# A fused retention and feed-forward kernel: one batch's transposes go from TensorE to the DMA, and its rows are worked off one group later

## Chip, cores and metric

One core of one Trainium2 chip. The metric is the device time of one execution in microseconds (us). Every ratio is the mean time of one kernel's fast runs over the mean of the fast runs of the kernel before in the same rounds, with a 95% interval, so it is not quite the ratio of the medians that are quoted beside it. A run counts as slow when it is over 1.5% above the fastest of the same kernel. The granted clock is the share of TensorE's full clock that the profile shows as allowed.

## The reference, cut to what matters

Four batches, eight heads, 768 positions and a head dimension of 64 go through a decayed linear attention. Its result (3072 rows of 512) goes through an RMS normalisation and a gated feed-forward network (FFN) with an inner width of 1536.

```python
def _attn_ref(q, k, v):
    ...
    for t in range(S):
        state = gamma[None, :, None, None] * state + np.einsum('bhd,bhe->bhde', k[:, :, t], v[:, :, t])
        y[:, :, t] = scale * np.einsum('bhd,bhde->bhe', q[:, :, t], state)

def _moe_ref(x, w_gate, w_val, w_out, rms_g):
    xn = x / np.sqrt(np.mean(x * x, axis=-1, keepdims=True) + 1e-06) * rms_g
    g = xn @ w_gate
    return (g * (1.0 / (1.0 + np.exp(-g))) * (xn @ w_val)) @ w_out
```

## The kernel before: the parts that matter here

The 768 positions are cut into six chunks of 128. A chunk of one batch, say (1,3) for chunk 1 and batch 3, passes through small pieces: load q, k, v (`load`), transpose q and k (`piece_t`), scores (`piece_a`), output and state (`piece_y`), scale of the norm (`piece_rstd`), normalise (`piece_n`), transpose for the FFN (`piece_x`). Group c is the FFN of chunk c for all four batches, which is 512 columns: twelve rows of gate and value matmuls (`gv`), then the down projection (`down`). The pieces of chunk c+1 are slotted between the rows of group c. For chunks 0 and 1 the transposes are done on TensorE, from chunk 2 on by the DMA:

```python
def piece_t(c, b):
    d = cur[c, b]
    if c > 1:
        for n in "qk":
            t = work.tile([128, NHP, 128], BF16, name=n + "T", bufs=8)
            nc.sync.dma_start_transpose(out=t, in_=d[n + "b"])
            d[n + "T"] = t
        return
    # ... else: eight transposes on TensorE into qk_ps, one copy into qkT

def piece_rstd(c, b):        # on GpSimd (POOL), in the same queue as the loads
    ms = work.tile([128, 1], F32, name="ms")
    nc.gpsimd.tensor_scalar(out=ms, in0=cur[c, b]["ssq"], ...)
    rstd = work.tile([128, 1], F32, name="rstd")
    nc.gpsimd.tensor_tensor(out=rstd, in0=ms, in1=mhalf, op=ALU.pow)

def piece_n(c, b):
    ...
    if c > 1:
        nc.vector.scalar_tensor_tensor(out=xn, in0=x, scalar=d["rstd"], in1=g_bc,
                                       op0=ALU.mult, op1=ALU.mult)
        nc.sync.dma_start_transpose(out=cur[c, "xnT"][:, :, b * C:(b + 1) * C], in_=xn)
        return
    # ... else: xn = x * rstd; piece_x transposes it on TensorE and applies g_col

def second(n):               # the first two rows of group 1
    gv(n, t=slice(0, GT - C))            # three batches, 384 columns
    if n == 0:
        piece_x(1, B - 1)                # xn of (1,3), on TensorE
    else:
        gv(0, 2, slice(GT - C, GT))      # the fourth batch of both rows, packed

AHEAD0 = {1: ((L, 1, 1),), 5: ((W, 0, 0),), 6: ((L, 1, 2),), 8: ((W, 0, 1),), 9: ((L, 1, 3),),
          10: ((W, 0, 2), (L, 2, 0)), 12: ((L, 2, 1),), 13: ((T, 2, 0),), 14: ((L, 2, 2),), 15: ((T, 2, 1),),
          16: ((L, 2, 3, "qk"),), 17: ((L, 2, 3, "v"),), 23: ((T, 2, 2),)}
```

`AHEAD0` says what is issued ahead in each slot of group 0: L loads a chunk and batch, T transposes it, W loads a third of the output weights. Loads are issued by POOL, transposes and outputs by SyncE (SP).

## Time and profile before

| | before |
|---|---|
| median of the first six runs | 234.71 us |
| profiled span, granted clock | 232.5 us, 1.0 |
| first row of group 1 starts | 58.32 us |
| last load of chunk 2 (v_f of (2,3)) issued, landed | 55.13, 67.43 us |
| first row of group 2 starts | 93.70 us |
| its last xnT transpose landed | 93.34 us |

The prediction shows the lines that carry the argument. From 33 us on TensorE (PE) has no gap. The DMA is full up to about 70 us. The transposes for group 2 land only 0.36 us before PE wants them (93.70 - 93.34).

### The profile page before, as it was taken

The numbers are of one execution on the slowest core, as the hardware profiler recorded it, in microseconds if no ns is written. First come the engines' busy times: TensorE is split into PE (matmuls) and PEld (weight loads), VectorE is DVE, ScalarE is ACT, GpSimd is POOL, SyncE is SP. The second block draws the span as 40 slices with busy tenths as digits, with TensorE's granted clock in tenths as the row PEclk, the third lists the DMA queues.
The fourth block names the chain that finished last, engine by engine and source line by source line (L and its number), as shares of the span: only waits on it lengthen the run. The fifth ranks groups of instructions, "written<-read, shape, count | busy, mean of one in ns | idle before, by whom it ended". The sixth has DMA issues, their size and how long they took to land.

```text
span 232.5 us, 4395 instructions
## 1 busy us (share of the span) xinstructions
PE 223.4 (96%) x1662; PEld 121.1 (52%) x1687; DVE 130.5 (56%) x220; ACT 93.6 (40%) x185; POOL 120.2 (52%) x181
## 2 busy tenths in 40 slices
PE   6789999999999999999999999999999999999994
PEld 4567567565645554445554445554445554444443
DVE  6775454998548892249793239793238582243300
ACT  7444676646533332433432332433332432433221
POOL 8969978787537789374749374649200211000000
PEclk9999999999999999999999999999999999999999
DMA  8999999999999799899895599697400025100022
GB/s 138 178 198 205 203 193 204 211 198 161 157 233 187 83 137 240 210 120 173 119 157 137 159 114 149 104 124 190 140 3 0 0 48 162 64 0 1 3 90 90
DMA packets 89013, 30.70 MB, mean 132 GB/s; under 512 B 78560, under 2 KB 84448, under 8 KB 88992
## 3 DMA queue, kind: packets, MB, share of 16 engines
q0 software_dynamic: 55488, 16.78, 69.8%
q1 hardware_dynamic: 32832, 13.57, 29.0%
q8 instruction: 13, 0.21, 0.4%
q10 hardware_dynamic: 672, 0.07, 0.2%
q14 instruction: 8, 0.07, 0.1%
HBM read 28.58 MB, written 6.29 MB: 150 GB/s over the span
## 4 chain that ended last, share of the span: by engine, by line
PE 86%; DMA 6%; POOL 4%; issue 1%; ACT 1%; DVE 1%; POOLq 0%; ACTq 0%
PE o_ps L400 25%; PE v_ps L349 25%; PE g_ps L349 25%; DMA wv_b<-in_moe_w_val_dram 3%; PE a_ps L215 3%; PE y_ps L233 2%; DMA kb<-in_k_dram 2%; PE y_ps L238 2%; PE kv_ps L264 2%; PE o_ps L390 1%; POOL qb L75 1%; POOL kb L75 1%; POOL v_f L75 1%; PE qk_ps L204 1%; PE xt_ps L306 1%
## 5 line engine op out<-in xcount | busy, mean ns | idle before, releaser
L354 DVE TENSOR_TENSOR hT<-sg,v_ps 128x512 bf16<-128x512 bf16 (+2 forms) x76 | 50.0, 658 | 77.8 <-PE v_ps L349 64.1
L349 PE MATMUL v_ps<-xnT,wv_b 128*128 128x512 bf16 (+3 forms) x343 | 74.1, 342 | 0.6 <-DMA wv_b<-in_moe_w_val_dram 0.3
L349 PE MATMUL g_ps<-xnT,wg_b 128*128 128x512 bf16 (+3 forms) x338 | 73.8, 342 | 0.7
L353 ACT ACTIVATE sg<-g_ps 128x512 bf16<-128x512 f32 (+2 forms) x76 | 43.6, 573 | 64.9 <-PE g_ps L349 60.0
L400 PE MATMUL o_ps<-wo_b,hT 128*128 128x512 bf16 x266 | 62.0, 379 | 0.5
L349 PEld LDWEIGHTS <-wv_b 128*128 128x128 bf16 x348 | 31.6, 98 | 31.3 <-DMA wv_b<-in_moe_w_val_dram 0.7
L349 PEld LDWEIGHTS <-wg_b 128*128 128x128 bf16 x348 | 30.2, 98 | 27.4 <-DVE xnT L307 0.7
L400 PEld LDWEIGHTS <-hT 128*128 128x128 bf16 x276 | 26.2, 98 | 28.5 <-DVE hT L354 0.2
L278 POOL TENSOR_SCALAR ms<-ssq 128x1 f32<-128x1 f32 x24 | 5.8, 241 | 49.5 <-ACT xsq L248 49.3
L75 POOL DMA_DIRECT2D qb<-in_q_dram x23 | 21.4, 931 | 11.6 <-PE v_ps L349 7.2
L221 DVE TENSOR_TENSOR am<-a_ps,causal 128x512 bf16<-128x512 f32 x40 | 24.9, 680 | 0.2
L405 ACT COPY o_sb<-o_ps 128x512 f32<-128x512 f32 x23 | 13.2, 583 | 29.1 <-PE o_ps L400 23.0
L248 ACT ACTIVATE xsq<-x 128x512 f32<-128x512 f32 x20 | 12.6, 630 | 29.9 <-DVE x L244 28.0
L182 POOL TENSOR_TENSOR vp<-v_f,vdec 128x512 bf16<-128x512 f32 x18 | 18.5, 1052 | 6.5 <-DMA v_f<-in_v_dram 6.3
L75 POOL DMA_DIRECT2D v_f<-in_v_dram x23 | 21.1, 917 | 0.4 <-issue 0.3
L75 POOL DMA_DIRECT2D kb<-in_k_dram x23 | 20.5, 890 | 0.6 <-PE v_ps L349 0.4
L244 DVE TENSOR_TENSOR x<-y_ps,ydec 128x512 f32<-128x512 f32 x20 | 13.7, 685 | 2.3 <-PE y_ps L238 2.0
L289 DVE SCALAR_TENSOR_TENSOR xn<-x,rstd,g_bc 128x512 bf16<-128x512 f32 x16 | 12.6, 786 | 3.5 <-POOL rstd L281 3.5
L281 POOL TENSOR_TENSOR rstd<-ms,mhalf 128x1 f32<-128x1 f32 x24 | 13.4, 557 | 2.0
L233 PEld LDWEIGHTS <-am 128*128 128x128 bf16 x192 | 8.8, 98 | 4.5
L274 POOL CAST st_b<-st_f 64x256 bf16<-64x256 f32 x24 | 10.5, 438 | 0.7
L256 DVE TENSOR_TENSOR st_f<-st_f,kv_ps 128x512 f32<-128x512 f32 x16 | 10.8, 676 | 0.0
(72 smaller groups left out, 149.3 us busy)
## 6 DMA issues: line engine op xcount, KB each, us to landing
v_f<-in_v_dram POOLq DMA_DIRECT2D x23, 256.0 KB, 6.7
out_dram<-o_sb SPq DMA_DIRECT2D x23, 256.0 KB, 2.3
qb<-in_q_dram POOLq DMA_DIRECT2D x23, 128.0 KB, 6.5
kb<-in_k_dram POOLq DMA_DIRECT2D x23, 128.0 KB, 6.4
wg_b<-in_moe_w_gate_dram POOLq DMA_DIRECT2D x4, 384.0 KB, 7.8
wv_b<-in_moe_w_val_dram POOLq DMA_DIRECT2D x4, 384.0 KB, 9.3
wo_b<-in_moe_w_out_dram POOLq DMA_DIRECT2D x3, 512.0 KB, 10.0
q_f<-in_q_dram SPq DMA_DIRECT2D x1, 256.0 KB, 3.6
```

The lines of the kernel that those rows point to most:

```text
L75: i = nc.gpsimd.dma_start(out=x, in_=dict(q=q, k=k, v=v)[n][b].rearrange("h (c p) d -> c p h d", p=C)[c])
L182: (nc.vector if (c, b) in VECTOR_V else nc.gpsimd).tensor_tensor(out=d["vp"], in0=d["v_f"], in1=vdec[:, c, :, None].to_broadcast([128, H, ...
L221: nc.vector.tensor_tensor(out=am[:, i], in0=a_ps[i], in1=mask, op=ALU.mult)
L233: nc.tensor.matmul(y_ps[:, h, :], d["am"][:, i, hp, :], d["vp"][:, h, :], start=first, stop=last, skip_group_check=True)
L244: nc.vector.tensor_tensor(out=x, in0=y_ps, in1=ydec[:, c, :, None].to_broadcast([128, H, D]), op=ALU.mult)
L248: nc.scalar.activation(xsq, x.rearrange("p h d -> p (h d)"), AF.Square, accum_out=ssq)
L281: nc.gpsimd.tensor_tensor(out=rstd, in0=ms, in1=mhalf, op=ALU.pow)
L349: cur["mm"] = nc.tensor.matmul(ps[:, n - n0, :], w_b[:, s, n * 128:(n + 1) * 128], xnT[:, s, t], start=s == 0, stop=s == KS - 1)
L353: nc.scalar.activation(sg, g_ps, AF.Silu)
L354: nc.vector.tensor_tensor(out=hT[:, n0:n1, t], in0=sg, in1=v_ps, op=ALU.mult)
L400: nc.tensor.matmul(o_ps, hT[:, n, b * C:(b + 1) * C], wo_b[:, n, :], start=n == 0, stop=n == NFF - 1)
L405: nc.scalar.copy(o_sb, o_ps)
```

## The change

Its intent is to take twelve transposes of batch (1,3) off the engine that bounds the kernel. q, k and the normalised xn of that batch go through the DMA. Its scores and output move from the end of group 0 into group 1. To give them time, group 1 does eight rows for three batches only (384 columns) and packs the fourth batch's part of these rows (128 columns, 64 matmuls: "the packed fourth") in after them. The DMA-transposed xn needs the norm's gain in a row layout (`g_bc`), so that load moves from group 1 to the start. The diff, cut to its core:

```diff
+    LATE = (1, B - 1)
...
     def piece_t(c, b):
-        if c > 1:
+        if c > 1 or (c, b) == LATE:
...
     def piece_n(c, b):
-        if c > 1:
+        if c > 1 or (c, b) == LATE:
...
-        def second(n):
-            gv(n, t=slice(0, GT - C))
-            if n == 0:
-                piece_x(1, B - 1)
+        def second(i):
+            if i < 6:
+                for n in ((0,), (1,), (2,), (3, 4), (5,), (6, 7))[i]:
+                    gv(n, t=slice(0, GT - C))
+            elif i < 8:
+                gv(4 * (i - 6), 4 * (i - 5), slice(GT - C, GT))
             else:
-                gv(0, 2, slice(GT - C, GT))
+                gv(i)
+            for f in {0: (piece_a,), 2: (piece_y,), 3: (piece_n,)}.get(i, ()):
+                f(*LATE)
...
-     ... 13: ((T, 2, 0),), ...
+     ... 13: ((T, 1, 3), (T, 2, 0)), ...
-    AHEAD1 = {0: (...), 1: ((T, 1, 3),), 3: ((V, 1, 3),), 4: ((L, 2, 0),), ...
+    AHEAD1 = {0: (...), 4: ((T, 1, 3), (V, 1, 3)), 5: ((L, 2, 0),), ...
...
-            if c == 1 and i == 4:
+            if c == 0 and i == NFF:
                 nc.sync.dma_start(out=g_bc, in_=moe_rms_g.partition_broadcast(128))
```

More of the change, by code (lines that the diff above doesn't have):

```diff
@@ L316 @@
     PLAN = dict(a=(5, 5, 9, 9), y=(7, 8, 11, 12), n=(9, 10, 13, 13))
-    PLAN1 = dict(v=(9, 12, 14, 17), t=(9, 11, 13, 16), a=(10, 12, 15, 18), y=(11, 14, 17, 20),
-                 n=(13, 16, 19, 22), x=(15, 18, 21, None))
+    PLAN1 = dict(v=(9, 12, 14, 17), t=(9, 11, 13, None), a=(10, 12, 15, None), y=(11, 14, 17, None),
+                 n=(13, 16, 19, None), x=(15, 18, 21, None))
     def attention(c):
@@ L373, in first @@
                 f(*x)
-        def second(n):
-            gv(n, t=slice(0, GT - C))
-            if n == 0:
-                piece_x(1, B - 1)
-            else:
-                gv(0, 2, slice(GT - C, GT))
+        def second(i):
[4 more added lines that the diff above has]
+                gv(4 * (i - 6), 4 * (i - 5), slice(GT - C, GT))
+            else:
+                gv(i)
+            for f in {0: (piece_a,), 2: (piece_y,), 3: (piece_n,)}.get(i, ()):
+                f(*LATE)
+            if i == 3:
+                cur.pop(LATE)
         o_t = {}
@@ L408, in ffn @@
         for n in range(NFF):
-            slots.append(lambda n=n: first(n) if c == 0 else second(n) if c == 1 and n < 2 else gv(n))
+            slots.append(lambda n=n: first(n) if c == 0 else second(n) if c == 1 else gv(n))
         if c == 0:
@@ L445 @@
     AHEAD0 = {1: ((L, 1, 1),), 5: ((W, 0, 0),), 6: ((L, 1, 2),), 8: ((W, 0, 1),), 9: ((L, 1, 3),),
-              10: ((W, 0, 2), (L, 2, 0)), 12: ((L, 2, 1),), 13: ((T, 2, 0),), 14: ((L, 2, 2),), 15: ((T, 2, 1),),
+              10: ((W, 0, 2), (L, 2, 0)), 12: ((L, 2, 1),), 13: ((T, 1, 3), (T, 2, 0)), 14: ((L, 2, 2),), 15: ((T, 2, 1),),
               16: ((L, 2, 3, "qk"),), 17: ((L, 2, 3, "v"),), 23: ((T, 2, 2),)}
-    AHEAD1 = {0: ((V, 1, 0), (V, 1, 1), (V, 1, 2)), 1: ((T, 1, 3),), 3: ((V, 1, 3),),
-              4: ((L, 2, 0),), 6: ((L, 2, 1),), 8: ((L, 2, 2),), 9: ((L, 2, 3),), 10: ((T, 2, 0),),
+    AHEAD1 = {0: ((V, 1, 0), (V, 1, 1), (V, 1, 2)), 4: ((T, 1, 3), (V, 1, 3)),
+              5: ((L, 2, 0),), 6: ((L, 2, 1),), 8: ((L, 2, 2),), 9: ((L, 2, 3),), 10: ((T, 2, 0),),
               13: ((V, 2, 0),), 14: ((V, 2, 1), (T, 2, 1)), 15: ((V, 2, 2), (V, 2, 3), (T, 2, 2))}
```

## The prediction

> **What bounds the kernel now.** I read, in this order, the busy shares, the 40 slices, the chain of work that ended last, the groups by shape, then the timeline from 25 to 95 us.
>
> ```profile
> PE 223.4 (96%) x1662; PEld 121.1 (52%) x1687; DVE 130.5 (56%) x220; ACT 93.6 (40%) x185; POOL 120.2 (52%) x181
> PE   6789999999999999999999999999999999999994
> DMA  8999999999999799899895599697400025100022
> PE 86%; DMA 6%; POOL 4%; issue 1%; ACT 1%; DVE 1%; POOLq 0%; ACTq 0%
> ```
>
> TensorE (PE) is the bound: from the fourth slice it shows no idle tenth, and the chain is 86% PE. The rest of the chain, DMA and POOL, lies before 33 us. But the DMA row is also full for the first dozen slices (to about 70 us), exactly where the change works. So a PE instruction removed is worth its start-to-start time, and a PE wait added is lost in full.
>
> The timeline of PE at the start of group 1 (columns: start us, us, engine, line, operation, tile, count) gives the spacing:
>
> ```profile
> 58.32 0.81 PE L349 MATMUL g_ps<-xnT,wg_b 128*128 128x384 bf16 x4
> 58.97 0.81 PE L349 MATMUL v_ps<-xnT,wv_b 128*128 128x384 bf16 x4
> 59.62 0.39 PE L306 MATMUL xt_ps<-ident,xn 128*128 128x128 bf16 x4
> ...
> 61.14 0.61 PE L349 MATMUL g_ps<-xnT,wg_b 128*128 128x128 bf16 x8
> 61.59 0.61 PE L349 MATMUL v_ps<-xnT,wv_b 128*128 128x128 bf16 x8
> ...
> 62.90 1.03 PE L349 MATMUL v_ps<-xnT,wv_b 128*128 128x512 bf16 x4
> ```
>
> Read the differences of the starts, not the durations, which overlap. Four 384-column matmuls take 58.97 - 58.32 = 0.65 us, eight of 128 columns 61.59 - 61.14 = 0.45 us (56 ns each), and four of 512 columns 0.865 us (62.90 to 63.76, the next group's start). Four transposes of xn take 0.22 us (59.62 to 59.84). Nothing is idle between.
>
> **What the Trainium skill says.** "TensorE: Matmul & The Clock Gate", section "Wait — 56ns, not 53.3ns?", gives a warm start-to-start of N / 2.4 GHz plus about 2.5 ns. The trace agrees: 56 ns for 128 columns, 216 ns for 512. So cutting a row into 384 + 128 costs only the added fixed parts. "DMA: Bandwidth & Descriptors", section "Issuing engines are not separate DMA queues", says that DMAs from SP and GpSimd share the same 16 engines and interleave. The trace agrees: between 50 and 60 us transposes issued by SP took 8.0 to 10.9 us to land, while in the quiet stretch 158 to 162 us they took 2.5 us. The same page, section "Anatomy of one DMA — SWDGE (gpsimd) path", says that a semaphore wait is done by the issuing sequencer and that the DMA engines only drain their queues. So a transfer with no wait starts as soon as its instruction is reached, whatever its place in the program text. No run yet shows it for g_bc.
>
> **The change part by part.**
> Removed from PE: eight transposes of q and k of batch (1,3), 8 x 56 = 0.44 us, and four of its xn, 0.22 us. Together 0.67 us.
> Added to PE: eight rows are cut into 384 + 128 instead of two. A cut row costs 2 x 0.65 + 0.445 = 1.745 us against 2 x 0.865 = 1.73 us for a whole one, so 0.015 us more; six more rows cost 0.09 us. Net PE work: -0.57 us.
> Removed elsewhere: an ACT copy of 1.01 us, a DVE eviction of 0.68 us; the xn operation becomes 0.74 instead of 0.48 us. Neither engine binds, so 0.
> Moved: scores (about 0.43 us with its gap), y and kv (0.68 us) of batch (1,3) go from the end of group 0 to slots 0 and 2 of group 1. With the q,k transposes (0.44) the end of group 0 becomes 1.55 us shorter.
> Added to DMA: two transposes near 46 us and one near 67 us. The hardware queue used 29.0% of 232.5 us, 67 us, for 13.57 MB; by bytes a 0.13 MB transpose is an estimated 0.65 us of all 16 engines.
> Moved in DMA: g_bc (256 KB). In the built kernel it is the fourth instruction of SP with no wait, so I expect it near 3 us instead of 69.5, among the first loads.
>
> Three waits can be exposed.
>
> (a) xn of batch (1,2). Its scale comes from GpSimd (POOL), which issues five loads in a row before it:
>
> ```profile
> 49.14 0.56 POOL L281 TENSOR_TENSOR rstd<-ms,mhalf 128x1 f32<-128x1 f32 x1
> 49.66 0.95 POOL L75 DMA_DIRECT2D qb<-in_q_dram  x1
> 50.61 0.89 POOL L75 DMA_DIRECT2D kb<-in_k_dram  x1
> 51.47 0.92 POOL L75 DMA_DIRECT2D v_f<-in_v_dram  x1
> 52.35 0.91 POOL L75 DMA_DIRECT2D qb<-in_q_dram  x1
> 53.38 0.88 POOL L75 DMA_DIRECT2D kb<-in_k_dram  x1
> 54.34 0.19 POOL L278 TENSOR_SCALAR ms<-ssq 128x1 f32<-128x1 f32 x1
> 54.61 0.56 POOL L281 TENSOR_TENSOR rstd<-ms,mhalf 128x1 f32<-128x1 f32 x1
> ```
>
> ```profile
> 55.20 0.48 DVE L296 TENSOR_SCALAR xn<-x,rstd 128x512 bf16<-128x512 f32 x1 [0.35 <-POOL rstd L281]
> 56.37 0.39 PE L306 MATMUL xt_ps<-ident,xn 128*128 128x128 bf16 x4
> ```
>
> POOL is busy without a pause, so xn is ready at 55.68 whatever PE does. Now PE comes at 56.37, 0.69 us later. In the changed kernel the same five loads stand before the same ms, and PE has lost all of the 1.55 us before this point: it arrives at 54.82. It must wait until about 55.75: +0.93 us. This I trust most; it eats the whole gain (-0.57 + 0.93 = +0.36).
> The loads also wait for earlier loads. With two more transposes in a full DMA, v_f of (2,0), landing at about 52.9, may come up to a microsecond later and hold the kb load that was issued at 53.38: I put +0.3 us.
>
> (b) g_bc at the start. PE already waits there for a weight load:
>
> ```profile
> 27.27 0.82 PE L349 MATMUL v_ps<-xnT,wv_b 128*128 128x384 bf16 x4 [0.27 <-DMA wv_b<-in_moe_w_val_dram]
> ```
>
> 256 KB at the 200 GB/s of these slices is 1.3 us, at the near 370 GB/s of 65 to 68 us 0.7 us. If the backlog lasts to 27 us it comes out here in full; I put +0.4 us for what reaches PE.
>
> (c) xnT of the late batch. Counting from a group start at 57.70: row 0, scores, rows 1 and 2 to 62.1; y and kv to 62.8; x (0.68), square (0.82) and rstd (0.75) to about 65.3; DVE is then held by the product of row 4, so xn is done at about 66.9. The packed fourth is wanted after eight rows (10.4), 1.1 of batch (1,3) and about 0.8 for two score pieces of chunk 2: 57.70 + 12.3 = 70.0. That leaves 3.1 us. Later xnT pairs landed in 2.5 to 6.2 us. In front of it on SP is this:
>
> ```profile
> 61.42 4.65 SPq L190 DMA_TRANSPOSE kT<-kb  x1
> ...
> 69.53 0.57 SPq L471 DMA_DIRECT2D g_bc<-in_moe_rms_g_dram  x1
> ```
>
> That kT took 8.9 us to land, at 70.3. So the wait is between 0 and 2 us; I put +0.4, leaning on the author having chosen eight rows to give it time.
>
> Sum: -0.57 + 0.93 + 0.3 + 0.4 + 0.4 = +1.46 us, on 234.76: **236.2 us**.
>
> **The rivals.**
> R1, all waits stay hidden: only the 0.57 us shows, 234.2 us. For it: PE is gapless, and the eight rows look chosen for the purpose. Against it: the POOL chain of (a) does not shorten.
> R2, only (a) bites: 234.76 + 0.36 = 235.1 us. For it: that chain is there line by line, while the DMA terms are guesses.
> R3, DMA becomes the bound for a stretch: (a) grows to 2, (b) to 0.7, (c) to 2 us: -0.57 + 4.7, 238.9 us. For it: a full DMA row and landings of 9 to 12 us. Against it: transposes share one queue behind each other, so they cannot take much at a time.
>
> **Range and chances.** The low end, 234.4, is R1 with the spread of the runs (234.32 to 235.98). The high end, 238.2, lies short of R3. Two per cent is 4.7 us: faster needs a gain eight times the removed work, 0.01; slower needs more than R3, 0.03; within, 0.96.
>
> **What would show it.** PE matmul busy time down by some 0.5 us. The first idle mark of PE after 50 us on xt (line 309), from DVE xn, about 0.9 us or more, with POOL busy before it. g_bc issued by SP near 3 us. A wait on wv_b near 27 us above 0.27. A wait of the first 16-fold 128-column g_ps in group 1 on the xnT transpose, 0 to 2 us. Groups 2 to 5 unchanged. I am wrong if xt does not wait (then POOL ran earlier than I hold) and the time falls by half a microsecond; or if the scores of (1,3) wait for qT and kT, which I expect to land by 57 us, two before they are wanted.

## The result, and the profile after

| | before | after |
|---|---|---|
| median of six runs | 234.71 us | 248.51 us |
| lowest and highest | 234.32, 235.98 | 242.33, 250.91 |
| ratio of fast runs | | 1.0349 [1.0291, 1.0407] |
| fast runs, their clock | all six | 242.33 and 243.76, clock 1.0 |
| the other five runs of after (one beyond the six) | | 246.75 to 250.91, clock 0.993 to 0.977 |

The changed kernel is slower by 3.5% in its fast runs, about 8.2 us. These are only two of seven; its median is 5.9% above that of before. The profile of after fell on its slowest run (250.91 us, clock 0.977). So the page shows where the waits are, but their sizes are read, as far as possible, from the experiments. The profiles of e5 and e7 below are of slow runs too.

The page of after (busy time and recorded instructions, PE, granted clock and DMA by fortieths of the span, shares of the chain):

```profile
PE 229.5 (92%) x1723; PEld 125.7 (50%) x1723; DVE 129.2 (52%) x220; ACT 92.8 (37%) x185; POOL 120.1 (48%) x181
PE   7679999996982999969999999999999999999994
PEclk9999999999997799979999999999999999999999
DMA  7999999999999929978999799999720004400022
PE 71%; DMA 16%; POOL 5%; ACT 2%; issue 2%; DVE 1%; POOLq 0%; ACTq 0%; DVEq 0%
```

PE now has holes in slices 10, 12, 13 and 18, and the clock falls in three slices that lie in or just behind the last two holes. The chain's DMA share went from 6% to 16%. Busy time is no measure of work here: a matmul at half clock counts twice, and some matmul records are missing from the page of before.

PE's timeline of after at the four places where it waits (start, us, engine, line, operation, tile, count, idle before and releaser; lines of the changed file are three higher):

```profile
9.64 0.40 PE L201 MATMUL qb_ps<-ident,qb 128*128 128x128 bf16 x4 [1.52 <-DMA qb<-in_q_dram]
...
59.08 0.40 PE L309 MATMUL xt_ps<-ident,xn 128*128 128x128 bf16 x4 [2.27 <-DVE xn L299]
...
79.48 1.89 PE L352 MATMUL g_ps<-xnT,wg_b 128*128 128x128 bf16 x16 [5.43 <-DMA xnT<-xn]
81.16 1.91 PE L352 MATMUL v_ps<-xnT,wv_b 128*128 128x128 bf16 x16
82.87 1.77 PE L352 MATMUL g_ps<-xnT,wg_b 128*128 128x128 bf16 x16
84.48 1.06 PE L352 MATMUL v_ps<-xnT,wv_b 128*128 128x128 bf16 x16
...
108.51 1.86 PE L352 MATMUL g_ps<-xnT,wg_b 128*128 128x512 bf16 x4 [2.33 <-DMA xnT<-xn]
```

The first is at the start and shifts everything by 1.85 us (the last 384-column gate row of chunk 0's start is followed by the packed rows at 34.95 us; before at 33.10). The second is xn of batch (1,2), the third the packed fourth, and the fourth the start of group 2, which before had begun without a wait at

```profile
93.70 1.03 PE L349 MATMUL g_ps<-xnT,wg_b 128*128 128x512 bf16 x4
```

Sixteen 128-column matmuls take 1.68 us from start to start at 79.48 (81.16 - 79.48), 105 ns each instead of 56: half clock. The packed fourth took 5.89 us (79.48 to 85.37) instead of some 3.58 (64 x 56 ns).

POOL's timeline of after shows what held xn and what held the rest of the loads:

```profile
54.40 0.89 POOL L75 DMA_DIRECT2D v_f<-in_v_dram  x1 [1.05 <-DMA qb<-in_q_dram]
55.27 0.88 POOL L75 DMA_DIRECT2D qb<-in_q_dram  x1
56.72 0.87 POOL L75 DMA_DIRECT2D kb<-in_k_dram  x1 [0.57 <-DMA v_f<-in_v_dram]
57.67 0.19 POOL L281 TENSOR_SCALAR ms<-ssq 128x1 f32<-128x1 f32 x1
...
68.38 1.04 POOL L185 TENSOR_TENSOR vp<-v_f,vdec 128x512 bf16<-128x512 f32 x1 [5.79 <-DMA v_f<-in_v_dram]
69.51 0.19 POOL L281 TENSOR_SCALAR ms<-ssq 128x1 f32<-128x1 f32 x1
...
78.51 1.04 POOL L185 TENSOR_TENSOR vp<-v_f,vdec 128x512 bf16<-128x512 f32 x1 [8.17 <-DMA v_f<-in_v_dram]
```

The ms of (1,2) stands at 57.67 instead of 54.34, behind two loads that each waited for an earlier load to land. The ms of the late batch (69.51) stands behind the value product of (2,2), which waited 5.79 us for its own load. The last load of chunk 2 landed at 78.36 us; before it was 67.43. That is the backlog that the rest of this document is about.

SP's timeline of after:

```profile
2.81 1.11 SPq L480 DMA_DIRECT2D g_bc<-in_moe_rms_g_dram  x1
...
68.37 3.66 SPq L193 DMA_TRANSPOSE kT<-kb  x1
73.18 1.27 SPq L294 DMA_TRANSPOSE xnT<-xn  x1
```

g_bc is issued among the first loads. The late xnT was ready on VectorE at 71.13, was issued after that kT at 73.18, and landed at 79.38 us.

### The profile page after: what moved, and what is told of

Read it like the earlier page. It is cut to its first block, busy times and chain, and to the rows that moved or that the text cites. A ratio compares the mean times of both kernels' runs of the same rounds, so it can differ in the third digit from the quotient of the medians.

```text
span 249.2 us, 4502 instructions
## 1 busy us (share of the span) xinstructions
PE 229.5 (92%) x1723; PEld 125.7 (50%) x1723; DVE 129.2 (52%) x220; ACT 92.8 (37%) x185; POOL 120.1 (48%) x181
## 4 chain that ended last, share of the span: by engine, by line
PE 71%; DMA 16%; POOL 5%; ACT 2%; issue 2%; DVE 1%; POOLq 0%; ACTq 0%; DVEq 0%
PE g_ps L352 23%; PE v_ps L352 23%; PE o_ps L409 17%; DMA xnT<-xn 5%; DMA v_f<-in_v_dram 4%; DMA qb<-in_q_dram 4%; DMA kb<-in_k_dram 3%; PE a_ps L218 2%; PE y_ps L236 2%; PE y_ps L241 1%; PE kv_ps L267 1%; ACT xsq L251 1%; POOL rstd L284 1%; PE o_ps L399 1%; POOL qb L75 1%
## 5 line engine op out<-in xcount | busy, mean ns | idle before, releaser
L352 PE MATMUL g_ps<-xnT,wg_b 128*128 128x512 bf16 (+3 forms) x372 | 77.4, 341 | 8.2 <-DMA xnT<-xn 7.8
L352 PE MATMUL v_ps<-xnT,wv_b 128*128 128x512 bf16 (+3 forms) x372 | 76.5, 337 | 0.0
L352 PEld LDWEIGHTS <-wg_b 128*128 128x128 bf16 x372 | 33.1, 102 | 35.3 <-DMA xnT<-xn 8.4
L352 PEld LDWEIGHTS <-wv_b 128*128 128x128 bf16 x372 | 34.0, 101 | 30.4 <-issue 1.1
L292 DVE SCALAR_TENSOR_TENSOR xn<-x,rstd,g_bc 128x512 bf16<-128x512 f32 x17 | 13.2, 778 | 4.5 <-POOL rstd L284 4.5
```

Source lines behind the costliest of these rows:

```text
L352: cur["mm"] = nc.tensor.matmul(ps[:, n - n0, :], w_b[:, s, n * 128:(n + 1) * 128], xnT[:, s, t], start=s == 0, stop=s == KS - 1)
```

## The experiments

Thirteen kernels ran in four batches (e1 to e4, e5 to e8, e9 to e11, e12 and e13), all with a correct result. The kernel before had medians of 234.59, 234.80, 235.47 and 235.19 us in them. "+us" below is the ratio minus one, times that median.

| run | what it is | median us | ratio of fast runs | +us |
|---|---|---|---|---|
| e1 | before, g_bc early | 236.25 | 1.0058 [1.0032, 1.0083] | 1.4 |
| e2 | after, g_bc held back to 42 us | 246.62 | 1.0499 [1.0467, 1.0531] | 11.7 |
| e3 | after's order, every transpose on PE, g_bc late | 238.83 | 1.0176 [1.0147, 1.0205] | 4.1 |
| e4 | after, idle matmuls before the packed fourth | 247.74 | 1.0534 [1.0489, 1.0579] | 12.5 |
| e5 | before, two idle DMA transposes | 241.31 | 1.0161 [1.0068, 1.0255] | 3.8 |
| e6 | after, q and k on PE | 240.37 | 1.0195 [1.0119, 1.0271] | 4.6 |
| e7 | after, POOL's loads late | 242.84 | 1.0220 [1.0132, 1.0308] | 5.2 |
| e8 | e3, POOL's loads late | 237.89 | 1.0115 [1.0060, 1.0170] | 2.7 |
| e9 | before, two idle plain copies | 237.37 | 1.0073 [1.0017, 1.0129] | 1.7 |
| e10 | e7, g_bc late | 241.01 | 1.0240 [1.0205, 1.0275] | 5.7 |
| e11 | e10, q and k on PE | 243.01 | 1.0299 [1.0226, 1.0372] | 7.0 |
| e12 | e10, late xnT first on SP | 239.80 | 1.0183 [1.0131, 1.0234] | 4.3 |
| e13 | e11, late xnT first on SP | 238.69 | 1.0156 [1.0105, 1.0206] | 3.7 |

### e1: g_bc at the start, alone

```diff
-            if c == 1 and i == 4:
+            if c == 0 and i == NFF:
                 nc.sync.dma_start(out=g_bc, in_=moe_rms_g.partition_broadcast(128))
```

> The kernel before, with only the g_bc load moved to where the changed kernel has it (no wait, so SP issues it near 3 us). Theory G (the early broadcast load delays the first q load of batch (0,1) from 4.8 to 6.6 us landing and shifts everything after it): PE waits about 1.5 us for qb near 8 to 10 us, the start of group 1 moves by about 1.85 us, time 236.6 us. Rival (the shift of the changed kernel at 35 us comes from elsewhere, or is absorbed by slack later): within 0.4 us of 234.7.

Measured: 236.25 us, 1.66 us above the median of before, 1.4 by the ratio, at clock 1.0 in all four runs. The packed rows of the start stand at 34.49 instead of 33.10 us, 1.39 us later. In the profile (of a run of 236.51 us) group 2 then waits as well:

```profile
95.98 1.02 PE L349 MATMUL g_ps<-xnT,wg_b 128*128 128x512 bf16 x4 [0.73 <-ACT o_sb L405]
```

It names ACT's copy, but the last xnT of group 2 had landed only at 95.85. Shown: 256 KB put among the first loads cost 1.4 to 1.7 us, where the prediction put 0.4, a quarter to a third of it. How much of this is the start and how much group 2 is not separated.

### e2: g_bc held back in the changed kernel

```diff
-                nc.sync.dma_start(out=g_bc, in_=moe_rms_g.partition_broadcast(128))
+                g_in = nc.sync.dma_start(out=g_bc, in_=moe_rms_g.partition_broadcast(128))
+                tc.add_manual_dep(g_in.ins, cur["mm"].ins.name, SYNC_DEP, reason="transfer order")
```

> The changed kernel with the g_bc load held until the matmuls of slot 11 of group 0 (about 43 us). Theory G: the first 35 us are as in the kernel before, so about 1.85 us less than the changed kernel's fast runs (242.3 to 243.8), about 240.5 to 242 us; xt still waits about 2 us and the packed fourth still waits 4 to 6 us for the xnT transpose, because those come from the transposes in a full DMA. Rival (the early shift is what puts PE and the transfers out of step): both later waits nearly vanish and the time is 235 to 236 us.

Measured: 246.62 us; neither expectation held. The early gain was there (a row of PE at 36.80 us, 36.69 before), but xt of (1,2) then waited 8.25 us at 63.33, with a stretch of half clock behind it, and the packed fourth waited only 0.20. Whether g_bc at 42 us is worse than at 3 us is not shown: all four runs (246.13 to 247.07) lie within the range of after's. What the run did show is a size: between the landing of the last output weights and that of qb of (2,0) lay 5.4 us, and 0.9 us before. In between were g_bc and the pair of transposes of (1,3). That led to e5.

### e3: the order of work alone

The changed kernel with `piece_t`'s and `piece_n`'s conditions put back to `c > 1`, the T of (1,3) in slot 23 of group 0, `piece_x` in slot 5 of group 1, and g_bc in its old place.

> The changed order of work (eight rows with three batches, batch (1,3) inside group 1, packed fourth), but q, k and xn of batch (1,3) are transposed on PE as before and g_bc is loaded where it was. No transfer is added. Theory T (the DMA transposes make the long waits): PE work is +0.09 us against before, xt of (1,2) waits about 0.9 us since POOL's chain is as in the kernel before, the packed fourth does not wait: 234.7 + 1.0 = 235.7 us, clock 1.0. Rival (the order of work itself makes the waits): 238 us or more.

Measured: 238.83 us, 4.1 us above before, where 235.7 was expected: a miss. With no transfer added, xt of (1,2) still waited 1.49 us, the scores just ahead of the packed fourth 0.71 (for the eviction of the late transpose), and group 2 1.25 us. PE's lines for the first and the last:

```profile
56.77 0.40 PE L309 MATMUL xt_ps<-ident,xn 128*128 128x128 bf16 x4 [1.49 <-DVE xn L299]
...
98.39 1.02 PE L352 MATMUL g_ps<-xnT,wg_b 128*128 128x512 bf16 x4 [1.25 <-DMA xnT<-xn]
```

So the reordering costs by itself. In the kernel before, batch (1,3)'s work stood ahead of xt and hid POOL's loads, and group 2's xnT had only 0.36 us to spare. Part of the 1.49 us is VectorE's (DVE):

```profile
55.39 1.32 DVE L299 TENSOR_SCALAR xn<-x,rstd 128x512 bf16<-128x512 f32 x1 [1.81 <-POOL rstd L284]
```

This xn took 1.32 us, and 0.48 in before. With 0.48 the wait would be an estimated 0.65 us (1.49 - 0.84). It took 1.3 us in e2, e4 and e6 too, but 0.49 in after; why is not shown.

### e4: idle matmuls to keep the clock up

```diff
+                if i == 6:
+                    fill_ps = fps.tile([128, 256], F32, name="fill_ps", tag="ff")
+                    for _ in range(36):
+                        nc.tensor.matmul(fill_ps, hot[:, 0:128], hot, start=True, stop=True)
```

> The changed kernel with 36 idle matmuls of 256 columns (about 4 us) in front of the packed fourth, where PE waits for xnT. Theory C (the slow runs of the changed kernel are the PE clock falling to half after the idle stretch of about 5 us): the wait is filled, the clock stays 1.0 there, the 64 packed matmuls take 56 ns instead of 105, and the runs lie at 242 to 244 us with few or none at 247 to 251. Rival (the slow runs have another cause): the runs spread as before, 242 to 251.

Measured: 247.74 us, inconclusive. In the profiled run the wait had moved to xt (3.69 us at 60.11, with a clock of 0.66 behind it); xnT had landed at 76.92, and the filling ran on to 80.12, so it cost some 3.2 us. The packed matmuls behind the filling did run at full speed (56 ns). This fits "an idle stretch lowers the clock", but a test by itself it is not.

### e5 and e9: the pair of transposes alone, and plain copies of the same size

e5 is the kernel before with two transposes that nothing reads, at slot 13 of group 0, where the changed kernel has its pair:

```diff
+    def idle_t(c, b):
+        for n in "qk":
+            t = work.tile([128, NHP, 128], BF16, name=n + "I", bufs=1)
+            nc.sync.dma_start_transpose(out=t, in_=cur[c, b][n + "b"])
...
-              ... 13: ((T, 2, 0),), ...
+              ... 13: ((T2, 1, 3), (T, 2, 0)), ...
```

> The kernel before, with two unused DMA transposes of q and k of batch (1,3) put on the hardware queue at slot 13 of group 0, just where the changed kernel issues its own pair; nothing reads them. Theory T (a pair of transposes in a full DMA holds the loads up by about 4.5 us, as the difference of 5.4 and 0.9 us between two landings in the gated run suggests): the loads of (2,0) land some 4 us later, POOL's v_f load waits for it, xn of batch (1,2) comes late and PE waits 1.5 to 4 us at xt, which it does not do in the kernel before: 237 to 239 us. Rival (the estimate by bytes that the prediction used: 1.3 us for the pair, of which the slack of 0.69 us hides half): 235.3 us or less.

e9 makes plain copies of them, as many bytes in 512 pieces of 256 bytes each:

```diff
-            t = work.tile([128, NHP, 128], BF16, name=n + "I", bufs=1)
-            nc.sync.dma_start_transpose(out=t, in_=cur[c, b][n + "b"])
+            t = work.tile([128, NHP, 136], BF16, name=n + "I", bufs=1)
+            nc.sync.dma_start(out=t[:, :, :128], in_=cur[c, b][n + "b"].rearrange("p (h d) -> p h d", h=NHP))
```

> The same as the run with the idle pair of transposes, but the two idle transfers are plain copies: the same source, 131 KB each, in 512 pieces of 256 bytes, as many bytes as the transposes and about as many packets (a transpose adds 544). Theory T (it is the transposing that is dear in a full DMA, not bytes or packets): qb of (2,0) lands at most 1 us later than in the kernel before, xt does not wait, 234.8 to 235.5 us. Rival (any 262 KB in small packets at this place costs it): qb lands 2 us or more later, group 2 waits for xnT, 237.5 to 239 us as with the transposes.

Measured, with landings from the DMA view of the profiled runs:

| | before | e9, copies | e5, transposes |
|---|---|---|---|
| qb of (2,0) landed | 50.63 | 50.82 | 53.07 |
| v_f of (2,3), the last of chunk 2, landed | 67.43 | 70.28 | 73.69 |
| group 2 waits | 0 | 0.25 | 3.79 |
| ratio of fast runs | 1 | 1.0073 | 1.0161 |

In e5, POOL's line shows the same wait as in after, and PE's line the end of it:

```profile
53.67 0.89 POOL L75 DMA_DIRECT2D v_f<-in_v_dram  x1 [1.78 <-DMA qb<-in_q_dram]
```

```profile
99.64 1.86 PE L349 MATMUL g_ps<-xnT,wg_b 128*128 128x512 bf16 x4 [3.79 <-DMA xnT<-xn]
```

Two transposes of 131 KB, which nothing waits for, make the kernel before 3.8 us slower by its two fast runs; the other two, 242.38 and 242.82 us, are slower still. The profile is of the 242.82 us run. There they delay the first load behind them by 2.4 us, not by the 4 that theory T had, and the end of chunk 2's loads by 6.3 us. POOL's later loads wait for earlier ones (1.78 us in the line above); how much of the growth from 2.4 to 6.3 us comes from that was not isolated. In that profile PE feels little of it at xt (0.87 us) and most of it 40 us later, at group 2. Theory T had the size and the wrong place; the estimate by bytes is refuted. The copies cost 1.7 us, between the two expectations. So 262 KB in small pieces on a full DMA cost something even as copies. That transposing costs more than copying these two runs do not show: the intervals of the two ratios overlap (1.0068 to 1.0255 and 1.0017 to 1.0129), and the landings (2.9 and 6.3 us later at the end) come from e9's fastest run and e5's slowest. Two fast profiles below support it: until 56 us e10 and e11 differ only by the real pair of (1,3). v_f of (2,1) landed at 55.16 us in e11 and at 59.27 in e10, 4.1 us later, where the copies moved it by 1.4 us (55.55 in before, 56.92 in e9). From 48 to 56 us, with the DMA full, it moved 127 GB/s in e10 and 177 in e11, but 194 in e9 and 174 in before.

### e6: only xn by DMA

The changed kernel with `piece_t`'s condition put back to `c > 1` and the T of (1,3) at slot 23.

> The changed kernel with q and k of batch (1,3) transposed on PE again (late in group 0); only its xn goes by DMA, and g_bc is loaded early as in the changed kernel. Beside the run that had all three on PE and g_bc late (238.8 us) this adds the early g_bc (+1.7 by the run on it) and the DMA transpose of xn. Theory T (the pair in group 0 is the main loss): xt waits under 2 us and the packed fourth under 1 us, 240 to 241 us. Rival (the late transpose of xn is the main loss, since it stands behind chunk 2's transposes on the queue whatever group 0 does): the packed fourth waits 3 to 5 us and the time is 243 to 246 us.

Measured: 240.37 us, as theory T had it, and the packed fourth did not wait. But that reading does not hold. In its profile PE was late already (the start's packed rows at 36.09 us, 34.95 in after; then 1.49 us of waiting at xt), so it reached the packed fourth at 74.27, after xnT had landed at 73.82. (Its clock was at half from 10.6 to 14.0 us, behind a wait of 1.61 us at the start.) e11 below shows the wait come back when PE is on time.

### e7 and e8: POOL's loads moved out of the way

```diff
-              ... 14: ((L, 2, 2),), 15: ((T, 2, 1),),
-              16: ((L, 2, 3, "qk"),), 17: ((L, 2, 3, "v"),), ...
+              ... 15: ((T, 2, 1),),
+              17: ((L, 2, 2), (L, 2, 3, "qk")), 18: ((L, 2, 3, "v"),), ...
```

> The changed kernel with the loads of batches (2,2) and (2,3) issued by POOL after the mean square of (1,2) instead of before it, so that no load stands in front of that xn. Theory P (POOL's queueing is what costs: xt waits only because POOL is held in a load): the wait at xt falls from 2.3 or more to under 0.3 us and the time by 2 to 4 us, to 239 to 243. Rival D (the full DMA sets the end: what is saved at xt is lost again at the packed fourth's xnT or at group 2): xt's wait is gone but the packed fourth waits 3 to 6 us, and the time is within 1.5 us of the changed kernel's in the same rounds' spirit, 245 to 249 us.

> The run with the changed order of work but every transpose on PE and g_bc late (238.8 us), with the same loads of (2,2) and (2,3) issued after the mean square of (1,2). Theory P: the 1.65 us wait at xt goes, 237.2 us, a little more than the kernel before for the waits on wv_b, xnT and group 2 that are left. Rival (the later loads only push chunk 2's transposes and so group 2's xnT back): group 2 waits 2 us or more instead of 1.25, 238.5 us or more.

Measured: both have no wait at xt any more, so it came from POOL's loads. e7 came to 242.84 us, inside theory P's range, although in its profile, of a slow run, the packed fourth waited 4.01 us as rival D had it: each was half right. e8 came to 237.89 us (expected 237.2), and what is left in its profile is 0.71 us for the eviction of the late transpose and group 2:

```profile
96.91 1.02 PE L352 MATMUL g_ps<-xnT,wg_b 128*128 128x512 bf16 x4 [1.30 <-DMA xnT<-xn]
```

So of the 4.1 us in e3, about 1.4 went with the wait at xt, the slow xn included (it took 0.49 us in e8; the intervals of the two ratios overlap).

### e10 and e11: g_bc late as well, with and without the pair

e10 is e7 with g_bc issued at slot 18 of group 0 (`c == 0 and i == 18`); e11 is e10 with q and k of (1,3) on PE.

> The changed kernel with both causes on POOL and at the start taken out: the loads of (2,2) and (2,3) after the mean square of (1,2), and g_bc issued at slot 18 of group 0. The pair of transposes in group 0 and the late xnT stay. If the parts add up: the run with late loads alone had a ratio of 1.022, less 0.006 for g_bc: 1.015 to 1.018, 238.3 to 239 us in fast runs. If the transposes' load on the DMA only moves its cost to another wait (packed fourth or group 2): 240 us or more.

> The last run without the pair of transposes in group 0 (q and k of (1,3) on PE), so of the change only the order of work and the DMA transpose of the late xn are left. Theory T: without that pair nothing waits for the late xnT, and the 0.7 us wait for the eviction of the PE transpose is gone too: 236.5 to 237.2 us, still above the kernel before because group 2's xnT is late. Rival (the order of work itself keeps costing): 237.9 us or more, as in the run with all transposes on PE and late loads.

Measured: 241.01 and 243.01 us. Both sums failed. Taking g_bc's 1.4 us out of e7 gained nothing, and taking the pair out as well did not help (the intervals of e10 and e11 overlap). PE's lines at the packed fourth, e10 and then e11:

```profile
73.33 1.07 PE L352 MATMUL g_ps<-xnT,wg_b 128*128 128x128 bf16 x16 [2.59 <-DMA xnT<-xn]
```

```profile
73.58 1.89 PE L352 MATMUL g_ps<-xnT,wg_b 128*128 128x128 bf16 x16 [3.66 <-DMA xnT<-xn]
```

Both start where xnT lands. What PE gained earlier, it waits here.

### e12 and e13: the late xnT put first on SP

In e6, e7, e10 and e11 that transpose landed at 73.3 to 74.9 us, whether it was issued at 67.0 or at 71.4. Two causes were open: it stands in SP's queue behind the transposes of (2,2), or the DMA as a whole is not through with chunk 2 until then. So the transposes of (2,2) were issued after it:

```diff
-              ... 23: ((T, 2, 2),)}
+              ... }
-    AHEAD1 = {..., 4: ((T, 1, 3), (V, 1, 3)), ...
+    AHEAD1 = {..., 4: ((T, 1, 2), (T, 1, 3), (V, 1, 3)), ...
```

> The run with g_bc and POOL's loads late (all transfers of the change kept), with the transposes of q and k of (2,2) issued after the late xnT instead of before it. Theory Q (place in the queue): xnT lands by 71 us instead of 73.3, the packed fourth waits under 0.8 us instead of 2.6, and the time falls by 1.5 to 2.5 us to about 238.5 us unless the scores of (2,2) or group 2 now wait. Rival D (the full DMA): xnT still lands within half a microsecond of the end of the v_f load of (2,3), at 72 us or later, the wait is 1.5 us or more, and the time stays within 1 us of 240.4.

> The same for the run without the pair of transposes in group 0. Theory Q: xnT lands by 70.5 us instead of 73.5, the packed fourth waits under 0.5 us instead of 3.7, 238.5 to 239.5 us instead of 241 to 243. Rival D: it lands at 72 us or later and the time stays at 240.5 us or more.

Measured: 239.80 and 238.69 us, 1.3 and 3.4 us less than e10 and e11 by the ratios (the intervals of e12 and e10 overlap a little, those of e13 and e11 do not). PE at the packed fourth, e12 and then e13:

```profile
72.63 1.07 PE L352 MATMUL g_ps<-xnT,wg_b 128*128 128x128 bf16 x16 [0.24 <-DMA xnT<-xn]
```

```profile
71.80 1.07 PE L352 MATMUL g_ps<-xnT,wg_b 128*128 128x128 bf16 x16 [1.58 <-DMA xnT<-xn]
```

The wait of e12 is not to be compared: in that profile PE was held 1.88 us at the start by a weight load, ran at half clock behind it and came late. The landings can be:

| run | v_f of (2,3) landed | late xnT issued | landed | packed fourth starts (wait) |
|---|---|---|---|---|
| after (slow run) | 78.36 | 73.18 | 79.38 | 79.48 (5.43) |
| e6 | 67.29 | 71.42 | 73.82 | 74.27 (none) |
| e7 (slow run) | 73.74 | 67.96 | 74.86 | 74.89 (4.01) |
| e10 | 69.98 | 68.89 | 73.29 | 73.33 (2.59) |
| e11 | 73.02 | 66.99 | 73.49 | 73.58 (3.66) |
| e12 | 71.96 | 69.47 | 72.57 | 72.63 (0.24) |
| e13 | 71.25 | 67.30 | 71.80 | 71.80 (1.58) |
| e8, xn on PE | 67.25 | | | 71.22 (0) |

Put first on SP, xnT still lands 0.6 us after the last load of chunk 2 (e12: 72.57 - 71.96; e13: 71.80 - 71.25), as it does in e11 (0.5), in e7 (1.1) and in after (1.0). In e10 the loads were done at 69.98, and there it landed 0.4 us behind the kT of (2,2) (72.85). It lands when the DMA has worked off what was issued before it, which points to the full DMA as the cause. In e6, where the loads were through before it was issued, it took 2.4 us; e12's 3.1 us is close to that, so there the late issue is most of it. Its place on SP is worth something too. Rival D had the mechanism and theory Q, for e13, the time.

## Why the prediction was wrong

Predicted 236.2 us (234.4 to 238.2) and "within 2%"; measured 248.51 in the median, 242.33 at best. Point by point:

**PE work, -0.57 us.** Not contradicted, but never visible: PE was not the bound while the DMA was behind.

**(a) xn of (1,2) behind POOL's loads, 0.93 us.** Right in place and mechanism: 2.27 us in after, "from DVE xn, about 0.9 us or more, with POOL busy before it". e3 without added transfers has 1.49 us, 0.84 of it from the slow xn; e7 and e8 take the loads away and the wait with them. The 0.3 us added for loads that wait for loads is where it goes wrong: POOL lost 1.05 + 0.57 us to them in after before that ms.

**(b) g_bc at the start, 0.4 us.** Right that it is issued there (at 2.81 us), mis-sized: 1.4 us by the ratio of e1. It did not come out at the wait on wv_b, as predicted, but in after at the first q load of batch 1 (1.52 us at 9.64).

**(c) The late xnT, 0.4 us.** Right in place, mis-sized: 2.59 us in a fast run (e10) and 5.43 in after's slow one. The prediction gave it "2.5 to 6.2 us" to land and 3.1 us of room, and then took the low end "leaning on the author having chosen eight rows". That is no evidence. In e7, e10, e11 and e13 it took 4.4 to 6.9 us.

**The steps that failed.** The first is the price of the added transfers: "by bytes a 0.13 MB transpose is an estimated 0.65 us of all 16 engines", and the sentence that dismissed rival R3, "transposes share one queue behind each other, so they cannot take much at a time". e5 measures the pair alone: 3.8 us on the kernel, and in its profile 6.3 us on the end of chunk 2's loads, against 1.3 us by bytes. The bytes were the wrong unit in a DMA that is full of small pieces; even plain copies in 256-byte pieces cost 1.7 us (e9). The second is the order of work. Without added transfers the prediction's terms come to 0.93 us for (a) and 0.09 for the cut rows; e3 measures 4.1 us, because waits came out at places that it had not followed: 0.71 us ahead of the packed fourth and 1.25 at group 2. Nor do the sizes of (b) and (c) go back to the pair: (b) is g_bc alone, and e11, without the pair, waits 3.66 us at (c).

**R3, "DMA becomes the bound for a stretch", 238.9 us,** was the rival that came nearest, with larger numbers; it had no term for group 2. The prediction gave "slower", which it said needs more than R3, a chance of 0.03.

**"Groups 2 to 5 unchanged".** Wrong. Group 2's xnT had 0.36 us to spare in the trace of before, and the chunk 3 loads begin when chunk 2's are through (68.51 before, 79.50 in after). Group 2 waits in all the profiles of e1 to e13 (0.25 to 3.79 us; in e1, e9 and e10 the profile names another releaser, but the last xnT landed only 0.1 us before the start there too) and 2.33 us in after.

**Not foreseen: the clock.** After an idle stretch PE ran at half speed for a while: in after the packed fourth took 2.3 us more for it (5.89 - 3.58). Apart from the start and the end of the kernel, such a stretch of half clock lasted 3.4 us or twice that in every profile that has one. After 25 us, the waits with half clock behind them were 3.66, 3.69, 3.79, 4.01, 5.43 and 8.25 us long, but also 2.33 (after) and 1.88 (e12); others of up to 2.59 us (e10) had none. The Trainium skill, "TensorE: Matmul & The Clock Gate", section "Why this matters for your kernels", warns of idle gaps over about 3 us; the traces agree but for those of 2.33 and 1.88. The clock explains only a part of the 8 us over which after's runs spread. The granted clock of the five slow runs (0.993 to 0.977 of spans of 245.0 to 249.2 us) is an estimated loss of at most 1.7 to 5.7 us, while their spans are 3.7 to 7.9 us above the mean of the two fast ones (241.35). The rest must be longer waits; which ones stays open, since only the slowest run was profiled and e4 settled nothing.

**The sum.** Single parts, each alone in the kernel before or in its plainest form: g_bc 1.4 (e1), the pair 3.8 (e5), the order of work with xn and all on PE 4.1 (e3). They add up to 9.3 us; the change costs 8.2. They do not simply add, as e10 and e11 show: what is gained before 71 us is given back there at the wait for the DMA. A version that beats the kernel before was not found; the best of the others, e8, which keeps the order and none of the transfers, is 1.2% slower.

**What stays open:** how the cost of the pair splits between small pieces and the transposing (the intervals overlap), how much of it POOL's waits add, why xn took 1.32 us in e3, and the drops of the clock after 1.88 and 2.33 us.

## What to carry to other kernels

Work taken off a busy engine and given to a DMA queue was not free here, where the DMA was full. Read the DMA row in the very slices where the change works, and when it is full, measure what one such transfer does to the landings behind it, by adding an idle one, before pricing it by bytes. Look also for the next stage's slack (here 0.36 us at group 2), because here a delay of loads showed up there, 40 us after its cause. If fixing one wait just makes the next one longer, the thing they both wait for is the bound.

## What the Trainium skill lacked or had wrong

- "Advanced Engine Details and Errata", section "X-Bar Transpose (TRN2)", says that transpose DMAs are as fast as regular DMAs and gives 350 to 400 GB/s. Beside a full stream of small loads, with a pair of 131 KB transposes in flight the DMA moved 127 GB/s from 48 to 56 us, without it 177 (e10, e11), and 194 with plain copies of the same bytes (e9). The pair alone cost the kernel 3.8 us, the copies 1.7 (e5, e9; the ratios' intervals overlap).
- No page that bears on this case prices a load put ahead of others that are wanted sooner: 256 KB of g_bc among the first loads cost 1.4 us (e1).
- "TensorE: Matmul & The Clock Gate", section "Why this matters for your kernels", puts the limit of a harmless gap at about 3 us. Here gaps of 1.88 (e12) and 2.33 us (after) were each followed by half clock for 3.4 us, while one of 2.59 us (e10) was not.
